# A lightweight convolution in front of a gated feed-forward: the first convolution by token steps, one cast moved, one pair of loads swapped

## The chip, the core and the metric

One NeuronCore of a Trainium2 chip runs the whole kernel in one launch. The metric is the device time of that launch in microseconds (us). Engines are named as the profile names them: PE is TensorE (matmuls; PEld are its weight loads), DVE is VectorE, ACT is ScalarE, POOL is GpSimd, SP is SyncE, which here only issues DMAs. A "q" behind an engine's name (SPq, POOLq) is its instruction queue, where DMA issues show. PSUM holds four tiles of 128 x 2 x 512 fp32 here; each is one buffer of a ring of four.

## The reference

Eight batches of 4096 tokens with 192 channels go through a causal convolution with 7 taps per head (8 heads of 24 channels, taps softmaxed), and the result through a feed-forward layer with a ReLU gate.

```python
w = softmax(weight)                                   # (8 heads, 7 taps)
out[b, s, h, g] = sum_k w[h, k] * x_pad[b, s + k, h, g]   # 6 zeros ahead of each sequence
x = out.reshape(32768, 192)
return (maximum(x @ w_gate, 0) * (x @ w_val)) @ w_out     # 192 -> 1536 -> 192
```

## The kernel before

**Units.** Batches b and b+4 are worked on as two streams; a unit `u` is 1024 tokens of both, two windows of 512 (`WIN`), and there are 16 units. A stream's channels lie in 64 partitions, so that the 128 partitions hold two streams; 192 channels are three chunks `c` of 64.

**Feed-forward.** For each unit and window, `gate_val` runs over `f`, the 12 blocks of 128 columns of `Wg` and `Wv`: twelve matmuls into two PSUM tiles, then ACT writes `gr` (ReLU), then DVE multiplies `gr` with the other tile into `hT`. For `f == 0` of the very first window the matmuls are ordered by chunk, so that chunk 0 can start before chunks 1 and 2 are there. `project_columns` multiplies by `Wo`.

**Convolution on PE (units 0 and 1).** x is cut into steps of 112 tokens; a step's matmul takes x itself as weights and a banded matrix of the taps (`bands[0]` for heads 0 to 3, `bands[1]` for heads 4 to 7) as moving data. `conv_dense(0, ...)` makes the first window: for each chunk in turn it takes one PSUM tile, does 40 matmuls (5 steps in the order `STEPS0` = 1, 0, 2, 3, 4, two heads' parts, two streams, two halves of the chunk) and evicts the tile to `xc[0]` (ACT for chunks 0 and 2, DVE for chunk 1). `conv_dense(1, [c])` makes the second window, one chunk ahead of each of the blocks f = 9, 10, 11 of the first window (`CONV1`). `conv(2)` and `conv(3)` make unit 1 in another form, with ACT copies into `y` and SP's DMA transposes into `xc[1]`.

**Convolution on the lane (units 2 to 14, here "the lane").** `lane_load(u)` loads a unit of x through POOL's queue into `x_e` (and, for unit 2, the last 16 tokens before it into `head`); `lane_turn(u)` has POOL copy `head` and `x_e` (into `turned` and `x_p`) and SP transpose them by DMA into `x_r`; ACT, DVE and POOL then form the sum over taps (`lane_first`, `product`, `lane_rest`, `add`). Unit 2's lane starts in unit 0, after `gate_val`, and its ACT and DVE work stands between unit 0's `gate_val` and unit 1's in the program order of these engines.

**The start.** SP loads the first window's x as five raw fp32 pieces (`load_raw`, order `STEPS0`); `cast` turns each into fp16: piece 1 half on POOL and half on ACT, pieces 0 and 2 on ACT, 3 and 4 on DVE. The weights are loaded by POOL's queue in five column slices (`load_w(0)` to `load_w(4)`, `Wg` and `Wv` each) into partitions 0 to 63 only; `both_halves` copies a slice to partitions 64 to 127: slices 0 and 1 on DVE, 2, 3 and 4 on POOL (`pool_halves`), and the last 256 columns by SP's DMA.

**What sets the order.** The schedule is manual: every engine runs its instructions in the order in which the program writes them. A tile framework puts in the semaphores. On POOL the order around the change is: four small fills (`ones`, two selects, `Z`, and `raw[0]`'s six zero rows, L160), the cast of piece 1's first half (L121), ten weight issues (L208), `pool_halves(2)` and `(3)` (L215), `load_x(1)` (L94, two issues), `pool_halves(4)`, `load_x(2)` (L94, two issues), `lane_load(2)` (L404 two issues, L415 one), the issue for `Wo` (L616), and then `lane_turn(2)`. `load_x(g)` loads the five steps of token group g for both streams, 2 x 5 x 128 rows of 192 elements; `lane_load` loads 2 x 8 x 128 such rows. On DVE the order is: band 0's eviction, the casts 3 and 4, the four copies for slices 0 and 1, the eviction of chunk 1, then `hT`. On ACT it is: the casts, `wn`, the cast of piece 2, band 1's eviction, the evictions of chunks 0 and 2, then `gr`. The three tiles of the first convolution are the first three buffers of the ring again, as in the order before the change.

Of the kernel before, what the change touches and what calls it, by code (L numbers as in the profile page):

```python
# [8 lines left out]
FP = mybir.dt.float32  # L9
# [6 lines left out]
def kernel(  # L16
# [12 lines left out]
    nc = tc.nc  # L29

    B, S, D = x.shape
    H, KW = weight.shape
    G = D // H
    DFF = moe_w_gate.shape[1]
    PAD = KW - 1
    NB = B // 2
    NCH = D // 64
    NBLK = D // 32
    NFF = DFF // 128
    WIN = 512  # L40
    NWIN = S // WIN
    SUB = 112
    STEPS = [4, 5, 4]
    TAPS = [(6, 5, 4), (3, 2), (1, 0)]
    GSUB = 5
    WARM = [2, 3, 1]
    STEPS0 = [1, 0, 2, 3, 4]
    CONV1 = [9, 10, 11]
# [8 lines left out]
    GROUPS = [(0, [WIN * w + SUB * j for j in range(GSUB)]) for w in range(2)]  # L57
    second = [min(t, 2 * UNIT - SUB) for t in range(UNIT, 2 * UNIT, SUB)]
# [11 lines left out]
    psum = ctx.enter_context(tc.tile_pool(name="psum", bufs=4, space=bass.MemoryType.PSUM))  # L70
# [5 lines left out]
    def staged(i, j):  # L76
        return stages[i][:, XH * j : XH * (j + 1)]

    def load_x(g, streams=range(2)):
# [22 lines left out]
    xts = {0: staged(0, 0).rearrange("p (j s d) -> p j s d", s=2, d=D)}  # L102
    ROWS = [SUB + PAD, 128, 128, 128, 80]
    raw = [
        apool.tile([128, FLAT - LDVE], FP, name=f"prod{jj + 1}")[:, 0 : 2 * D] for jj in range(GSUB)
    ]
# [10 lines left out]
            ),  # L117
        )

    def cast(copy, jj, lo=0, hi=2 * D):  # L120
        copy(  # L121
            out=xts[0][0 : ROWS[jj], jj, :, :].rearrange("p s d -> p (s d)")[:, lo:hi],
            in_=raw[jj][0 : ROWS[jj], lo:hi],
        )

    HR = 128 // H
# [35 lines left out]
    with nc.allow_low_precision("one of the terms is not zero"):  # L162
        nc.vector.tensor_reduce(
            out=Z[:, 112 : 112 + HR],
            in_=eye[:].rearrange("p (g i) -> p i g", i=HR),
# [4 lines left out]
        out=mask[:, :, 0],  # L170
        in_=eye[:].rearrange("p (g i) -> p g i", i=HR),
# [17 lines left out]
    for half in range(2):  # L189
        nc.tensor.matmul(  # L190
            out=raised[half][:, 0, 0 : SUB * H // 2],
            lhsT=zeros[:, 0:128],
            rhs=zeros[:, 0 : SUB * H // 2],
            start=True,
            stop=False,
            skip_group_check=True,
# [16 lines left out]
    def both_halves(copy, s, dst):  # L213
        cols = slice(HALVES[s], HALVES[s + 1])
        copy(out=dst[64:128, :, cols], in_=dst[0:64, :, cols])  # L215
# [2 lines left out]
        both_halves(nc.gpsimd.tensor_copy, s, Wg)  # L218
        both_halves(nc.gpsimd.tensor_copy, s, Wv)

    cast(nc.gpsimd.tensor_copy, 1, 0, D)
    for s in range(5):
        load_w(s)
    pool_halves(2)
# [6 lines left out]
        out=mx[:], in_=spread[:, 0, 0:KW], axis=mybir.AxisListType.X, op=ALU.max, negate=True  # L231
    )
    nc.scalar.activation(out=e[:, 0:KW], in_=spread[:, 0, 0:KW], func=ACTF.Exp, bias=mx[:])
    cast(nc.scalar.copy, 1, D)
    cast(nc.scalar.copy, 0)
    prod = const.tile([128, BW, KW], FP)
    z0 = Z[:, 112 - PAD : 113 - PAD]
# [2 lines left out]
        out=prod[:],  # L240
# [11 lines left out]
        out=blocks[:],  # L252
# [11 lines left out]
    for half, copy in enumerate((nc.vector.tensor_copy, nc.scalar.copy)):  # L264
        for j in range(128 // HR):
            s0 = HR * j - PAD
            lo, hi = max(0, -s0), min(BW, SUB - s0)
            nc.tensor.matmul(
                out=raised[half][:, 0, 0 : SUB * H // 2].rearrange("p (h t) -> p h t", t=SUB)[
                    :, :, s0 + lo : s0 + hi  # L270
                ],
                lhsT=Z[:, 112 - HR * j : 240 - HR * j],
                rhs=blocks[:, H // 2 * half : H // 2 * (half + 1), lo:hi],
                start=False,
                stop=(j == 128 // HR - 1),
                skip_group_check=True,
            )
        copy(
            out=bands[half][:].rearrange("p h t -> p (h t)"), in_=raised[half][:, 0, 0 : SUB * H // 2]
# [7 lines left out]
    for c in range(NCH):  # L287
        r0 = 0
        while r0 < 64:
            h = (64 * c + r0) // G  # L290
            r1 = min(64, G * (h + 1) - 64 * c)
            row = wn[HR * h : HR * h + 8, :]
            for st in range(2):
                nc.sync.dma_start(
                    out=tap[64 * st + r0 : 64 * st + r1, c, :],
                    in_=bass.AP(
                        tensor=row.tensor,
                        offset=row.offset,
                        ap=[row.ap[0], [0, (r1 - r0) // 8], [1, KW]],
                    ),  # L300
# [6 lines left out]
    def band(h):  # L307
        return bands[h // 4][0 : SUB + PAD, h % 4, :]

    xc = {}  # L310
# [3 lines left out]
    PLACE = {0: (0, 0, 0), 1: (0, 0, 1), 3: (0, 1, 0), 4: (0, 1, 1)}  # L314
    PLACE |= {6: (1, 0, 0), 7: (1, 0, 1), 2: (1, 1, 0), 5: (1, 1, 1)}

    def conv_dense(g, chunks):


        xt = xts[g]  # L320
        t0 = GROUPS[g][1][0]
        rows = SUB + PAD
        for c in chunks:
            ps = psum.tile([128, 2, 512], FP, name="ps")
            for jj in STEPS0:
                col = SUB * jj
                n = min(SUB, WIN - col)
                rows = n + PAD
                for second in range(2):
                    for st in range(2):  # L330
                        for k2 in range(2):
                            k = 2 * c + k2
                            h0, h1 = 32 * k // G, (32 * k + 31) // G
                            h, m = (h0, G * h1 - 32 * k) if second else (h1, 32)
                            p0 = 64 * st + 32 * k2
                            nc.tensor.matmul(
                                out=ps[p0 : p0 + m, 0, col : col + n],
                                lhsT=xt[0:rows, jj, st, 32 * k : 32 * k + m],
                                rhs=band(h)[0:rows, 0:n],
                                start=True,  # L340
                                stop=True,
                                tile_position=(0, p0),
                                skip_group_check=True,
                            )
            copy = nc.vector.tensor_copy if c == 1 and g == 0 else nc.scalar.copy
            copy(out=xc[0][:, c, t0 : t0 + WIN], in_=ps[:, 0, :])  # L346

    def conv(g):

# [47 lines left out]
    def lane_load(u):  # L397


        bp, t0 = u * UNIT // S, u * UNIT % S  # L400
        xe = epool.tile([128, TILES, 2, NCH, 64], F16, name="x_e")
        for st in range(2):
            row = (bp + NB * st) * S + t0
            nc.gpsimd.dma_start(  # L404
                out=xe[:, :, st, :, :].rearrange("p j c r -> p j (c r)"),
                in_=bass.AP(
                    tensor=x.tensor,
                    offset=x.offset + row * D,
                    ap=[[D, 128], [128 * D, TILES], [1, D]],
                ),  # L410
            )
        head = None
        if t0 and u - 1 not in xes and u - 1 not in xrs:
            head = const.tile([HALO, 2, NCH, 64], F16, name="head")
            nc.gpsimd.dma_start(  # L415
                out=head[:].rearrange("p s c r -> p s (c r)"),
                in_=bass.AP(
                    tensor=x.tensor,
                    offset=x.offset + (bp * S + t0 - HALO) * D,
                    ap=[[D, HALO], [NB * S * D, 2], [1, D]],  # L420
                ),
            )
        xes[u] = xe, head
# [95 lines left out]
    def gate_val(u, w):  # L519
        h = hpool.tile([128, NFF, 2, WIN], F16, name="hT")  # L520
        xcb = xc[u]
        for f in range(NFF):
            if u == 0 and w == 0 and f in CONV1:
                conv_dense(1, [CONV1.index(f)])
            pss = [psum.tile([128, 2, 512], FP, name="ps") for _ in range(2)]
            order = [(i, c) for i in range(2) for c in range(NCH)]
            if u == 0 and w == 0 and f == 0:
                order.sort(key=lambda ic: ic[1])
            for i, c in order:
                W = (Wg, Wv)[i]  # L530
                for st in range(2):
                    nc.tensor.matmul(  # L532
                        out=pss[i][:, st, :],
                        lhsT=W[64 * st : 64 * st + 64, c, 128 * f : 128 * (f + 1)],
                        rhs=xcb[64 * st : 64 * st + 64, c, WIN * w : WIN * (w + 1)],
                        start=(c == 0),
                        stop=(c == NCH - 1),
                        tile_position=(64 * st, 0),
                    )
            gr = gpool.tile([128, 2, WIN], F16, name="gr")  # L540
            nc.scalar.activation(out=gr[:], in_=pss[0][:], func=ACTF.Relu)  # L541
            nc.vector.tensor_tensor(out=h[:, f], in0=gr[:], in1=pss[1][:], op=ALU.mult)  # L542
        return h
# [62 lines left out]


    xc[0] = xcpool.tile([128, NCH, UNIT], F16, name="xc")
    both_halves(nc.vector.tensor_copy, 0, Wg)
    both_halves(nc.vector.tensor_copy, 0, Wv)  # L610
    both_halves(nc.vector.tensor_copy, 1, Wg)
    both_halves(nc.vector.tensor_copy, 1, Wv)
    conv_dense(0, range(NCH))
    xts[2] = load_x(2)
    lane_load(2)
    nc.gpsimd.dma_start(out=Wo[:], in_=moe_w_out.rearrange("(c p) d -> p c d", p=128))  # L616
    for u in range(NUNIT):
        lane = 1 <= u < NUNIT - 1
# [12 lines left out]
        if lane:  # L631
            for k in range(4 if u == 1 else 2, KW - 1):
                add(u + 1, k)
        hs = [gate_val(u, w) for w in range(2)]
        if lane:
            add(u + 1, KW - 1)
# [14 lines left out]
        for p in range(3):  # L651
            ps = project_columns(hs, p)
# [39 lines left out]
```

## Time and profile before

| what | value |
|---|---|
| median of 3 runs | 770.39 us (768.64 to 770.94) |
| the profiled execution's own time | 771.82 us |
| its span, first to last instruction | 770.1 us |
| PE busy | 761.8 us (99%) |
| DVE, ACT, POOL busy | 87%, 78%, 55% |
| granted PE clock | 1.0 |

The profile is of one execution, and its times count from the start of its span. A row of the timeline gives start, duration, engine, line, operation, tiles and count, and in brackets the idle time just before it with what ended it. A row of the chain of work that ended last gives start, duration and what the time went into. A "DMA share" is the mean busy share of the core's 16 DMA engines; it can be over 1 where transfers of one engine overlap.

### The profile page before, as it was taken

How to read it: one execution, taken by the hardware profiler on the slowest of the kernel's cores; microseconds unless marked ns; L12 is line 12 of the kernel's file. 1: busy time of each engine (PE TensorE's matmuls, PEld its weight loads, DVE VectorE, ACT ScalarE, POOL GpSimd, SP SyncE). 2: the span in 40 equal slices, each digit the busy share in tenths (PEclk: the TensorE clock that was granted, in tenths of full speed). 3: DMA queues.
4: the chain of work that ended last, by engine and by line, in shares of the span. 5: the costliest groups of instructions: out<-in, count | busy, mean ns of one | idle time of the engine just before them, and what ended most of it. 6: DMA issues, size and time to landing. Idle time of an engine off the chain costs nothing.

```text
span 770.1 us, 21550 instructions
## 1 busy us (share of the span) xinstructions
PE 761.8 (99%) x9402; PEld 380.9 (49%) x9402; DVE 669.9 (87%) x630; ACT 598.1 (78%) x622; POOL 423.1 (55%) x191
## 2 busy tenths in 40 slices
PE   8999999999999999999999999999999999999998
PEld 5454544444444444444444444444444444444448
DVE  6778989989899898989989899898998989996690
ACT  6788787978879787787878879788796877874471
POOL 8506839286490955919368292863919558191000
PEclk9999999999999999999999999999999999999999
DMA  8946919084290914709066190742909232040402
GB/s 131 127 78 106 124 28 141 2 113 53 56 112 3 140 26 80 87 3 149 18 97 70 23 144 2 116 51 48 118 3 133 33 76 50 2 83 2 83 2 83
DMA packets 123214, 53.79 MB, mean 70 GB/s; under 512 B 87648, under 2 KB 123120, under 8 KB 123120
## 3 DMA queue, kind: packets, MB, share of 16 engines
q1 hardware_dynamic: 86192, 38.06, 31.3%
q0 software_dynamic: 36768, 14.26, 17.8%
q8 instruction: 73, 1.20, 0.6%
q14 instruction: 21, 0.17, 0.1%
q10 hardware_dynamic: 160, 0.10, 0.0%
HBM read 29.40 MB, written 25.17 MB: 71 GB/s over the span
## 4 chain that ended last, share of the span: by engine, by line
PE 91%; POOL 3%; ACT 2%; DMA 1%; issue 1%; SPq 1%; DVE 0%; ACTq 0%; POOLq 0%
PE ps L532 60%; PE ps L552 28%; PE ps L588 2%; ACT prod L469 1%; SPq L443 1%; DMA Wg<-in_moe_w_gate_dram 1%; DMA x_r<-x_p 1%; POOL out_s L94 0%; POOL Wg L215 0%; POOL Wv L215 0%; POOL x_p L441 0%; DMA prod<-in_x_dram 0%; POOL x_e L404 0%; ACT out_s L371 0%; ACT acc L489 0%
## 5 line engine op out<-in xcount | busy, mean ns | idle before, releaser
L541 ACT ACTIVATE gr<-ps 128x1024 f16<-128x1024 f32 x384 | 392.6, 1023 | 146.7 <-PE ps L532 146.6
L542 DVE TENSOR_TENSOR hT<-gr,ps 128x1024 f16<-128x1024 f16 x384 | 468.6, 1221 | 42.2 <-ACT gr L541 15.8
L478 POOL TENSOR_TENSOR prod<-prod,prod 128x1792 f32<-128x1792 f32 x70 | 278.4, 3977 | 254.8 <-DVE prod L510 211.8
L532 PE MATMUL ps<-xc,Wg 64*128 64x512 f16 x2304 | 313.3, 376 | 2.0 <-DVE xc L346 1.0
L532 PE MATMUL ps<-xc,Wv 64*128 64x512 f16 x2304 | 312.8, 376 | 0.4 <-DVE hT L542 0.4
L552 PE MATMUL ps<-hT,Wo 128*32 128x512 f16 x4320 | 236.0, 379 | 0.0
L532 PEld LDWEIGHTS <-Wv 64*128 64x128 f16 x2304 | 131.0, 94 | 118.4 <-issue 1.2
L532 PEld LDWEIGHTS <-Wg 64*128 64x128 f16 x2304 | 113.3, 94 | 139.1 <-issue 8.9
L552 PEld LDWEIGHTS <-Wo 128*32 128x32 f16 x4320 | 114.1, 97 | 120.3 <-issue 6.3
L469 ACT ACTIVATE prod<-x_r,tap 128x1024 f32<-128x1024 f16 (+1 forms) x182 | 172.8, 1037 | 0.2 <-POOL xc L478 0.2
L500 DVE SCALAR_TENSOR_TENSOR acc<-x_r,tap,acc 128x1024 f32<-128x1024 f16 (+1 forms) x140 | 114.2, 873 | 5.6 <-ACT acc L489 5.6
L566 DVE STREAM_TRANSPOSE out_s<-ps 128x1024 f32<-128x1024 f32 x45 | 56.1, 1247 | 30.9 <-PE ps L552 30.8
L478 POOL TENSOR_TENSOR xc<-prod,prod 128x1792 f16<-128x1792 f32 x14 | 55.7, 3981 | 1.1
L441 POOL COPY x_p<-x_e 128x1536 f16<-128x1536 f16 x28 | 40.3, 1468 | 2.3 <-DMA x_e<-in_x_dram 2.3
L404 POOL DMA_DIRECT2D x_e<-in_x_dram x28 | 25.1, 901 | 4.2 <-POOL x_p L441 4.2
L489 ACT ACTIVATE acc<-x_r,tap 128x1024 f32<-128x1024 f16 (+1 forms) x28 | 21.5, 820 | 3.6 <-DMA x_r<-x_p 3.6
L500 DVE SCALAR_TENSOR_TENSOR xc<-x_r,tap,acc 128x1024 f16<-128x1024 f16 (+1 forms) x28 | 23.4, 877 | 0.0
L588 PE MATMUL ps<-Wo,hT 128*128 128x192 f16 x192 | 16.0, 246 | 0.0
L588 PEld LDWEIGHTS <-hT 128*128 128x128 f16 x192 | 15.8, 98 | 0.4 <-issue 0.4
L599 ACT COPY out_s<-ps 128x768 f32<-128x768 f32 (+2 forms) x5 | 3.2, 639 | 12.7 <-PE ps L588 12.7
L599 DVE COPY out_s<-ps 128x192 f32<-128x192 f32 x1 | 0.4, 358 | 13.3 <-PE ps L588 13.3
L510 DVE TENSOR_SCALAR prod<-x_r,tap 128x768 f32<-128x768 f16 x14 | 8.6, 612 | 0.0
(56 smaller groups left out, 61.3 us busy)
## 6 DMA issues: line engine op xcount, KB each, us to landing
out_dram<-out_s SPq DMA_DIRECT2D x63, 384.0 KB
x_e<-in_x_dram POOLq DMA_DIRECT2D x28, 384.0 KB, 10.2
x_r<-x_p SPq DMA_TRANSPOSE x112
out_s<-in_x_dram POOLq DMA_DIRECT2D x4, 240.0 KB, 5.6
prod<-in_x_dram SPq DMA_DIRECT2D x3, 192.0 KB
Wo<-in_moe_w_out_dram POOLq DMA_DIRECT2D x1, 576.0 KB, 11.7
out_s<-in_x_dram POOLq DMA_DIRECT2D x2, 192.0 KB, 4.9
Wg<-in_moe_w_gate_dram POOLq DMA_DIRECT2D x1, 240.0 KB, 5.7
```

What stands on the lines that cost most here:

```text
L404: nc.gpsimd.dma_start(out=xe[:, :, st, :, :].rearrange("p j c r -> p j (c r)"), in_=bass.AP(tensor=x.tensor, offset=x.offset + row * D, ap ...
L441: nc.gpsimd.tensor_copy(out=xp[:, :, :, st, :], in_=xe[:, :, st, :, :])
L469: nc.scalar.activation(out=prods[u, k][:, at - LDVE : at - LDVE + n], in_=shifted(u, c, k, t, n), func=ACTF.Copy, scale=tap[:, c, k : k + 1],)
L478: nc.gpsimd.tensor_tensor(out=p0[:] if k < KW - 1 else flat(u)[:, LDVE:FLAT], in0=p0[:], in1=prods.pop((u, k))[:], op=ALU.add,)
L489: nc.scalar.activation(out=accs[u][:, at : at + n], in_=shifted(u, c, 0, t, n), func=ACTF.Copy, scale=tap[:, c, 0:1],)
L500: nc.vector.scalar_tensor_tensor(out=(flat(u) if k == KW - 1 else acc)[:, at : at + n], in0=shifted(u, c, k, t, n), scalar=tap[:, c, k : k ...
L532: nc.tensor.matmul(out=pss[i][:, st, :], lhsT=W[64 * st : 64 * st + 64, c, 128 * f : 128 * (f + 1)], rhs=xcb[64 * st : 64 * st + 64, c, WI ...
L541: nc.scalar.activation(out=gr[:], in_=pss[0][:], func=ACTF.Relu)
L542: nc.vector.tensor_tensor(out=h[:, f], in0=gr[:], in1=pss[1][:], op=ALU.mult)
L552: nc.tensor.matmul(out=ps[32 * s : 32 * s + 32, b, :], lhsT=Wo[:, f, 64 * p + 32 * b : 64 * p + 32 * b + 32], rhs=hs[s // 2][:, f, s % 2, ...
L566: nc.vector.transpose(out=o[:, :, 64 * p : 64 * p + 64].rearrange("p t (b c) -> p b t c", b=2), in_=ps[:].rearrange("p b (t c) -> p b t c" ...
L588: nc.tensor.matmul(out=ps[:, i // 2, D * (i % 2) : D * (i % 2) + D], lhsT=h[:, f, st, 128 * q : 128 * (q + 1)], rhs=Wo[:, f, :], start=(f ...
```

## The change

Three things change, all of them in the first 30 us of the program's order.

1. The first convolution allocates its three PSUM tiles at once and runs by steps instead of by chunks: steps 1, 0, 2 of chunks 0, 1, 2, then step 3 of all chunks, then step 4 of all chunks. The number of matmuls stays 120. The three evictions stand at its end. On DVE, slice 0's two copies stand ahead of the eviction of chunk 1 and slice 1's two copies behind it. The function is split into `conv_steps` and `evict`; the second window's convolution uses the same two in the order that it had.
2. POOL casts nothing: ACT casts the whole of piece 1. POOL's ten weight issues then follow its small fills directly.
3. On POOL's queue `lane_load(2)` (with `head`) stands ahead of `load_x(2)`.

```diff
-    cast(nc.gpsimd.tensor_copy, 1, 0, D)
     for s in range(5):
         load_w(s)
...
-    cast(nc.scalar.copy, 1, D)
+    cast(nc.scalar.copy, 1)
     cast(nc.scalar.copy, 0)
...
-    def conv_dense(g, chunks):
...
-        for c in chunks:
-            ps = psum.tile([128, 2, 512], FP, name="ps")
-            for jj in STEPS0:
...
-            copy = nc.vector.tensor_copy if c == 1 and g == 0 else nc.scalar.copy
-            copy(out=xc[0][:, c, t0 : t0 + WIN], in_=ps[:, 0, :])
+    def conv_steps(g, ps, c, steps):
+        for jj in steps:
...
+    def evict(copy, g, ps, c):
+        copy(out=xc[0][:, c, WIN * g : WIN * (g + 1)], in_=ps[:, 0, :])
...
             if u == 0 and w == 0 and f in CONV1:
-                conv_dense(1, [CONV1.index(f)])
+                c = CONV1.index(f)
+                ps = psum.tile([128, 2, 512], FP, name="ps")
+                conv_steps(1, ps, c, range(GSUB))
+                evict(nc.scalar.copy, 1, ps, c)
...
     xc[0] = xcpool.tile([128, NCH, UNIT], F16, name="xc")
+    first = [psum.tile([128, 2, 512], FP, name="ps") for _ in range(NCH)]
+    for steps in (STEPS0[:3], STEPS0[3:4], STEPS0[4:]):
+        for c in range(NCH):
+            conv_steps(0, first[c], c, steps)
     both_halves(nc.vector.tensor_copy, 0, Wg)
     both_halves(nc.vector.tensor_copy, 0, Wv)
+    for c, copy in enumerate((nc.scalar.copy, nc.vector.tensor_copy, nc.scalar.copy)):
+        evict(copy, 0, first[c], c)
     both_halves(nc.vector.tensor_copy, 1, Wg)
     both_halves(nc.vector.tensor_copy, 1, Wv)
-    conv_dense(0, range(NCH))
+    lane_load(2)
     xts[2] = load_x(2)
-    lane_load(2)
     nc.gpsimd.dma_start(out=Wo[:], in_=moe_w_out.rearrange("(c p) d -> p c d", p=128))
```

More of the change, by code (lines that the diff above doesn't have):

```diff
@@ L118, in load_raw, with cast @@
         )
-    def cast(copy, jj, lo=0, hi=2 * D):
+    def cast(copy, jj):
         copy(
-            out=xts[0][0 : ROWS[jj], jj, :, :].rearrange("p s d -> p (s d)")[:, lo:hi],
-            in_=raw[jj][0 : ROWS[jj], lo:hi],
+            out=xts[0][0 : ROWS[jj], jj, :, :].rearrange("p s d -> p (s d)"),
+            in_=raw[jj][0 : ROWS[jj], :],
         )
@@ L315 @@
     PLACE |= {6: (1, 0, 0), 7: (1, 0, 1), 2: (1, 1, 0), 5: (1, 1, 1)}
-    def conv_dense(g, chunks):
-        xt = xts[g]
-        t0 = GROUPS[g][1][0]
-        rows = SUB + PAD
-        for c in chunks:
-            ps = psum.tile([128, 2, 512], FP, name="ps")
-            for jj in STEPS0:
[L326 to L344, printed above, removed]
-            copy = nc.vector.tensor_copy if c == 1 and g == 0 else nc.scalar.copy
-            copy(out=xc[0][:, c, t0 : t0 + WIN], in_=ps[:, 0, :])
@@ new lines, in conv_steps @@
+    def conv_steps(g, ps, c, steps):
+        for jj in steps:
+            col = SUB * jj
+            n = min(SUB, WIN - col)
+            rows = n + PAD
+            for second in range(2):
+                for st in range(2):
+                    for k2 in range(2):
+                        k = 2 * c + k2
+                        h0, h1 = 32 * k // G, (32 * k + 31) // G
+                        h, m = (h0, G * h1 - 32 * k) if second else (h1, 32)
+                        p0 = 64 * st + 32 * k2
+                        nc.tensor.matmul(
+                            out=ps[p0 : p0 + m, 0, col : col + n],
+                            lhsT=xts[g][0:rows, jj, st, 32 * k : 32 * k + m],
+                            rhs=band(h)[0:rows, 0:n],
+                            start=True,
+                            stop=True,
+                            tile_position=(0, p0),
+                            skip_group_check=True,
+                        )
```

## The prediction

> **What bounds the kernel now.** I read the page's engine row first, then PE's waits and the timeline where PE stands still, and then the chain of work that ended last, for the first 72 us.
>
> ```profile
> PE 761.8 (99%) x9402; PEld 380.9 (49%) x9402; DVE 669.9 (87%) x630; ACT 598.1 (78%) x622; POOL 423.1 (55%) x191
> ```
>
> PE is busy in 761.8 of 770.1 us. The change takes no work off PE, so only PE's standstills can be won.
>
> The timeline places them, each with its wait in brackets:
>
> ```profile
> 9.64 0.39 PE L532 MATMUL ps<-xc,Wg 64*128 64x512 f16 x2 [1.01 <-DVE xc L346]
> 10.50 0.83 PE L532 MATMUL ps<-xc,Wg 64*128 64x512 f16 x6
> 12.17 0.33 PEld L532 LDWEIGHTS <-Wg 64*128 64x128 f16 x5 [0.50 <-POOL Wg L215]
> 12.94 0.33 PEld L532 LDWEIGHTS <-Wv 64*128 64x128 f16 x5 [0.44 <-POOL Wv L215]
> 21.46 0.23 PE L336 MATMUL ps<-band,out_s 118*32 118x112 f16 x2
> 22.63 0.63 PE L336 MATMUL ps<-band,out_s 118*32 118x112 f16 x38 [0.94 <-DMA out_s<-in_x_dram]
> 61.80 0.82 PE L532 MATMUL ps<-xc,Wg 64*128 64x512 f16 x6
> 65.71 0.82 PE L532 MATMUL ps<-xc,Wg 64*128 64x512 f16 x6 [0.96 <-ACT gr L541]
> 66.97 0.82 PE L532 MATMUL ps<-xc,Wv 64*128 64x512 f16 x6 [0.43 <-DVE hT L542]
> ```
>
> PE first waits for chunk 1 (until 9.64), then for POOL's copies of slice 2 (12.17, 12.94), then for the second window's x, which `load_x(1)` brings (22.63), and last in unit 1 for ACT and DVE, 0.96 + 0.43 = 1.39 us. So two stretches matter: up to 22.63, which ends with a landing, and up to 66.97. The chain tells what sets both:
>
> ```profile
> 3.44 0.47 POOL out_s L121
> ...
> 6.62 4.54 DMA Wg<-in_moe_w_gate_dram
> ...
> 11.30 0.82 POOL Wg L215
> ...
> 15.07 1.73 POOL out_s L94 x2
> ...
> 19.03 1.66 POOL out_s L94 x2
> ...
> 24.06 7.66 issue
> ...
> 35.21 1.59 SPq L443
> ...
> 44.75 4.04 DMA x_r<-x_p
> ...
> 64.64 1.03 ACT gr L541
> ```
>
> It is one POOL chain: weight issues, slice 2's landing (11.16), POOL's copies, `load_x(1)` at 15.07, the loads behind it, the landing of `head` (31.7), POOL's copies, SP's transposes, `x_r` (seen by ACT at 49.10), ACT's products, and the late `gr` at 64.64.
>
> **The cast off POOL (term A).** POOL's last fill ends at 1.88 + 0.41 = 2.29 us, and its weight issues begin at 3.91, behind the wait for piece 1 and the cast:
>
> ```profile
> 1.88 0.41 POOL L160 MEMSET prod<- 6x384 f32 x1
> 3.40 0.99 ACT L121 CAST out_s<-prod 128x192 f16<-128x192 f32 x2
> 5.57 0.51 ACT L121 CAST out_s<-prod 128x384 f16<-128x384 f32 x1 [0.85 <-DMA prod<-in_x_dram]
> ```
>
> All ten issues can come 3.91 - 2.29 = 1.6 us earlier. On ACT the first of the two casts in 0.99 grows to the 0.51 of a full one, by some 0.03 to 0.16 us; `wn` and the tap issues behind it on SP shift by that. The taps' first reader is ACT at 49.10, and the two `both_halves` issues behind them on SP feed f = 10 and 11, so this costs nothing.
>
> How much of the 1.6 us lasts until slice 2 lands? The x pieces (SP's queue, q1) and the weights (POOL's, q0) share the DMA engines. The rows are of the view of DMA queues (packets, MB, share of the engines' time), in this order for 0 to 4.0 us, 4.0 to 5.2, 5.5 to 8.1 and 24 to 31; a row of POOL's issues from the timeline stands last:
>
> ```profile
> q1 hardware_dynamic: 677, 0.49, 43.9%
> q1 hardware_dynamic: 458, 0.33, 89.1%
> q0 software_dynamic: 839, 0.20, 86.3%
> q0 software_dynamic: 3052, 1.15, 147.9%
> 6.62 0.63 POOL L208 DMA_DIRECT2D Wg<-in_moe_w_gate_dram  x1
> ```
>
> x nearly alone takes a share of 0.89, the first weights nearly alone 0.86, and a longer stretch later 1.48. So 0.9 isn't the ceiling; both at full rate would want 1.75, and at 1.48 each keeps 85%. The first weights move 839 / 2.6 = 323 packets per us, hardly more than POOL hands out (an issue of 64 x 3 rows takes 0.63 us, 305 per us): that stretch waits for the issues, and an earlier issue pays. At 85% during the overlap I take 1.2 us of the 1.6 as kept. The bounds are 0 (the slowest engine never idle, total work the same) and 1.6; it is nearer the upper because of the 1.48.
>
> It could be less: if an engine serves the two queues in turn and overlaps nothing, a pair of packets costs 16 x 0.89 / 382 = 37 ns (x: 458 / 1.2 per us) plus 16 x 0.863 / 323 = 43 ns, so either queue gets 200 per us instead of 323. Some 500 of the 1152 x rows are left at 4.0 us (q1's first row, less its few other packets) and take until 6.5; 268 of the 768 rows of slices 0 and 1 remain then and end at 7.3 instead of 8.1. That keeps 0.8 us: a rival of its own below. (The Trainium skill, "DMA: Bandwidth & Descriptors", section "Queues, rings and completion order", says that each DMA engine takes turns between the queues that have work, a packet at a time, which speaks for this price; no row here shows both queues busy for long enough to bear it out.)
>
> x pieces that come later: piece 2 delays ACT's cast and, behind it, band 1's eviction; pieces 3 and 4 delay DVE's casts and, behind them, slice 0's copies. By the turns the last x row comes 1.1 us later, step 4 is cast at about 8.0, and the convolution ends at 8.4. PE has this to spare, as the next part shows.
>
> **The convolution by steps.**
>
> ```profile
> 6.31 1.78 PE L336 MATMUL ps<-band,out_s 118*32 118x112 f16 x120 [0.18 <-DVE band L278]
> 7.24 0.58 ACT L346 CAST xc<-ps 128x512 f16<-128x512 f32 x1 [0.72 <-PE ps L336]
> 8.34 0.58 ACT L346 CAST xc<-ps 128x512 f16<-128x512 f32 x1 [0.52 <-PE ps L336]
> 8.58 0.28 DVE L215 COPY Wv<-Wv 64x384 f16<-64x384 f16 x1
> 8.90 0.69 DVE L346 CAST xc<-ps 128x512 f16<-128x512 f32 x1
> ```
>
> The same 120 matmuls end at 8.1. Chunk 0 loses: its eviction moves from 7.24 to about 8.1. Chunk 1 wins: it now stands ahead of slice 1's copies on DVE (8.58), so it runs 8.2 to 8.9 instead of 8.90 to 9.59. ACT evicts chunk 2 at 8.7 to 9.3. PE does f = 0 chunk by chunk at (10.50 - 9.64) / 2 = 0.43 us each: 8.75, 9.18, 9.61, and f = 1 starts at 10.05 instead of 10.50. Slice 1's copies (4 x 0.28 us for both slices) are now queued behind the eviction, 8.9 to 9.5, in time for f = 1. With slice 2's copies 1.2 us earlier (done at 10.9 and 11.7) f = 2 at 11.35 no longer waits. A block takes 12.88 / 10 = 1.29 us:
>
> ```profile
> 29.05 12.88 DVE L542 TENSOR_TENSOR hT<-gr,ps 128x1024 f16<-128x1024 f16 x10 [0.75 <-ACT gr L541]
> ```
>
> So PE reaches the second window's convolution at 10.05 + 8 x 1.29 = 20.4 instead of 21.46.
>
> But there it needs `load_x(1)`'s second stream, which lands 22.63 - 1.2 = 21.4 if it moves with POOL's chain. **So the step order alone is worth nothing here; the landing decides, and term A is 1.2 us.** Without the head start the wait at 22.63 would merely grow. From the other side, PE's own path allows at most about 22.63 - 20.6 = 2.0, if the load lands earlier still (it would move partly ahead of SP's copies of the last columns).
>
> **The lane's load first (term B).** `head` and `x_e` leave POOL's queue 1.66 us earlier in issue and no longer stand behind the 1280 rows of `load_x(2)`: 3052 / 7 = 436 rows per us makes 2.9 us. With A, `head` lands at 31.7 - 4.1 = 27.6, and `turned`, `x_p`, the transposes (35.21 becomes 31.1) and `x_r` (49.10 becomes 45.0) follow. ACT is free of `conv(2)`'s copies at 49.10 - 2.33 = 46.77, in the new frame 45.6, so its wait of 2.33 us goes:
>
> ```profile
> 44.11 1.03 PE L358 MATMUL ps<-out_s,band 118*112 118x240 f16 x8
> 45.07 5.36 PE L552 MATMUL ps<-hT,Wo 128*32 128x512 f16 x96
> 49.10 1.55 ACT L489 ACTIVATE acc<-x_r,tap 128x1024 f32<-128x1024 f16 x2 [2.33 <-DMA x_r<-x_p]
> 62.63 1.24 DVE L566 STREAM_TRANSPOSE out_s<-ps 128x1024 f32<-128x1024 f32 x1
> Wo<-in_moe_w_out_dram POOLq DMA_DIRECT2D x1, 576.0 KB, 11.7
> ```
>
> PE asks for the first `gr` of unit 1 about 0.9 us after 61.80, at 62.7; ACT gives it at 64.64, 1.9 late. Winning 2.3 covers that. DVE, fed by the same accumulators, is free after its last transpose (62.63) at about 63.6, which then waits for PE alone; it is then just in time, so I leave 0.1 and count **1.3 of the 1.39 us**. Bounds: 0, if `x_r` isn't earlier, and 1.39.
>
> What moves back is `load_x(2)`: two issues behind three others, landing by about 31.7, where `lane_load(2)` landed. `conv(2)` reads it at 44.11: 12 us of cover. `Wo` keeps its place; it lands 11.7 us after its issue at 23.0 and is read at 45.07. `load_x(3)`'s issues come earlier with the POOL copies and cost nothing.
>
> **Sum.** 1.2 + 1.3 = 2.5 us off the profiled 771.82 gives 769.3. That execution lies 1.4 us above the median of the runs; the same 2.5 off 770.39 gives 767.9.
>
> **Rivals.**
> 1. *Engines take turns between the queues* (above): A is 0.8, and the time 770.39 - 2.1 = 768.3.
> 2. *The head start is lost*: the slowest DMA engine was never idle, slice 2 lands at 11.1 as before. For it: the landing took 4.54 us after the issue. Against: the issue-limited rate. Only B stays: 769.1; with some of A, 768.7.
> 3. *The lane isn't earlier* (something else holds ACT): A alone, 769.2. Against: the chain goes through that wait.
> 4. *Slower: SP's transposes collide with loads.* They now start at 31.1, while `Wo` and `load_x(2)` still move. SP's transposes are spread between
>
> ```profile
> L443 SPq DMA_TRANSPOSE x_r<-x_p x8: 1246/1254/1594, 35.2 to 44.7; - x8
> L390 SPq DMA_TRANSPOSE xc<-out_s x10: 1175/1252/2023, 46.8 to 65.1; - x10
> ```
>
> 1.25 and 2.02 us an issue. Eight at 2.02 from 31.1 and a landing of 4.04 give 51.3, against 47.9 for an `x_r` that keeps its place relative to PE: 3.4 us lost on ACT, 1.2 won by A, 772.6. It turns from gain to loss where 31.1 + 8s + 4.04 passes 49.10, at s = 1.75. Against: the old transposes ran into `load_x(3)` and seven of the eight kept near 1.25.
>
> **How the numbers follow.** Chances: forecast 0.45; turns 0.17; head start lost 0.14; lane not earlier 0.10; collision 0.14. About 0.3%, 2.3 us, is what can be told from no change, so faster means under 768.1: the forecast lies just beyond that, and with A between 1.0 and 2.0 its own range is 767.1 to 768.1, so nearly all of it counts (0.42); half of the turns (0.08) and a little of the others (0.02) make it 0.52. Slower by that, over 772.7, is the collision's worse part, 0.09; between lies 0.39. The range goes from 766.4 (A at 2.0, B at 1.39, and 0.6 for the spread of the runs) to 770.6 (half of the collision left out, and nothing won).
>
> **What would show it.** POOL's first weight issue at about 2.3; slice 2's copy at about 10.1 instead of 11.30; f = 1 on PE at about 10.1; the convolution of the second window resuming at about 21.4 with a wait of about 0.8; `turned` at about 27.6 instead of 31.74; no wait of ACT ahead of `acc`; no PE wait for `gr` in unit 1. It is wrong if slice 2's copies don't move, if x pieces come so late that the convolution ends after 9.5, if the transposes stretch beyond 1.75 us, or if PE meets a new wait behind 67 us.

## The result, and the profile after

| | before | after |
|---|---|---|
| median, 7 runs each | 770.63 us (768.64 to 772.18) | 768.55 us (767.80 to 768.68) |
| profiled execution, its own time | 771.82 us | 768.63 us |
| its span | 770.1 us | 766.9 us |

The ratio is 0.9973, with a 95% interval of 0.9961 to 0.9985: 2.1 us less, a shade under the 0.3% that the prediction took as the bound. The two profiled executions lie 3.2 us apart.

The engine row and PE's waits of the changed kernel, from the page and from the view of waits:

```profile
PE 761.4 (99%) x9402; PEld 378.6 (49%) x9402; DVE 670.9 (87%) x630; ACT 598.6 (78%) x622; POOL 422.9 (55%) x190
```

```profile
PE ps L180 <- DVE e L136: 1.3, 1, 1.3
PE ps L530 <- ACT xc L341: 0.6, 1, 0.6
PE ps L530 <- DVE hT L540: 0.2, 1, 0.2
```

PE's work is the same, and the waits for the second window's x and for unit 1's `gr` and `hT` are gone. The timeline of the changed kernel at the places that the prediction named:

```profile
2.25 0.85 POOL L208 DMA_DIRECT2D Wg<-in_moe_w_gate_dram  x1
6.61 0.77 DVE L121 CAST out_s<-prod 128x384 f16<-128x384 f32 x2 [0.43 <-DMA prod<-in_x_dram]
8.55 1.07 ACT L341 CAST xc<-ps 128x512 f16<-128x512 f32 x2 [1.87 <-PE ps L330]
8.79 0.82 POOL L215 COPY Wg<-Wg 64x768 f16<-64x768 f16 x1
10.48 0.83 PE L530 MATMUL ps<-xc,Wg 64*128 64x512 f16 x6
12.81 0.82 PE L530 MATMUL ps<-xc,Wv 64*128 64x512 f16 x6 [0.21 <-DVE hT L540]
21.34 0.64 PE L330 MATMUL ps<-band,out_s 118*32 118x112 f16 x40
25.86 0.62 POOL L430 COPY turned<-head 16x192 f16<-16x192 f16 x2 [3.87 <-DMA head<-in_x_dram]
29.33 11.15 SPq L438 DMA_TRANSPOSE x_r<-x_p  x8
45.33 1.59 ACT L484 ACTIVATE acc<-x_r,tap 128x1024 f32<-128x1024 f16 x2
60.51 0.82 PE L530 MATMUL ps<-xc,Wg 64*128 64x512 f16 x6
64.41 0.81 PE L530 MATMUL ps<-xc,Wg 64*128 64x512 f16 x6
```

and one further row of before, unit 1's fourth block:

```profile
67.61 0.83 PE L532 MATMUL ps<-xc,Wg 64*128 64x512 f16 x6
```

The 3.2 us of this pair come in two steps. Unit 1 starts at 60.51 instead of 61.80, which is 1.29 us, and its fourth block at 64.41 instead of 67.61, which is 1.91 us more. From there on the two keep that distance. Of the 1.29 us only some 0.1 lies ahead of the second window's convolution (21.34 against 21.46); the rest is before's wait there, until 22.63. The chain that ended last tells how the work moved:

```profile
6.46 2.06 PE ps L330 x89
8.53 0.02 issue
8.55 0.60 ACT xc L341
9.15 0.04 issue
9.19 1.27 PE ps L530 x10
10.46 0.02 issue
10.48 1.03 ACT gr L539
11.52 0.02 issue
11.54 1.23 DVE hT L540
12.77 0.04 issue
12.81 8.59 PE ps L530 x78
```

Before, the chain ran through POOL, a landing, SP's transposes and ACT up to 66.97. Now it is PE's own from 12.81 on. Just ahead of that lies one detour: block f = 2 needs the PSUM tile that `hT` of f = 0 gives back at 12.77.

### The profile page after: what moved, and what is told of

The parts are those of the page before. It is cut to its first block, busy times and chain, and to the rows that moved or that the text cites. A ratio compares the mean times of both kernels' runs of the same rounds, so it can differ in the third digit from the quotient of the medians.

```text
span 766.9 us, 21548 instructions
## 1 busy us (share of the span) xinstructions
PE 761.4 (99%) x9402; PEld 378.6 (49%) x9402; DVE 670.9 (87%) x630; ACT 598.6 (78%) x622; POOL 422.9 (55%) x190
## 4 chain that ended last, share of the span: by engine, by line
PE 99%; ACT 0%; POOL 0%; DVE 0%; issue 0%; POOLq 0%
PE ps L530 65%; PE ps L550 31%; PE ps L586 2%; PE ps L330 0%; PE ps L353 0%; PE ps L180 0%; DVE hT L540 0%; ACT gr L539 0%; PE ps L267 0%; PE ps L190 0%; ACT xc L341 0%; PE ps L186 0%; POOL prod L160 0%; POOL rows L144 0%; ACT out_s L597 0%
## 5 line engine op out<-in xcount | busy, mean ns | idle before, releaser
L530 PEld LDWEIGHTS <-Wg 64*128 64x128 f16 x2304 | 111.2, 94 | 138.8 <-issue 6.9
```

The source lines that it names most:

```text
L530: nc.tensor.matmul(out=pss[i][:, st, :], lhsT=W[64 * st : 64 * st + 64, c, 128 * f : 128 * (f + 1)], rhs=xcb[64 * st : 64 * st + 64, c, WI ...
```

## The experiments

The theories: (1) the end is the later of two chains, PE's path up to the second window's convolution and the lane's chain; (2) two independent sums, A and B. Beside them stood the question what the order by steps is worth. The first six kernels are the other six combinations of the three parts.

**The cast alone.**

```diff
-    cast(nc.gpsimd.tensor_copy, 1, 0, D)
...
-    cast(nc.scalar.copy, 1, D)
+    cast(nc.scalar.copy, 1)
```

> The kernel before with only the cast of piece 1 taken off POOL. Theory 1 (the end is the later of two chains: PE's own path up to the second window's convolution, and the lane's chain POOL, head, transposes, ACT products): POOL's chain comes about 2.1 us earlier as in the changed kernel, the second window no longer makes PE wait, PE gains 1.3 to 1.6 us up to 23 us, and its wait in unit 1 shrinks because the lane's chain gains more than PE: in all about 2 us, 768.6. Theory 2 (two independent sums, A = 1.3 and B = 1.9): A alone, 769.3, with the full waits of unit 1. On the step order: theory 1 expects f = 1 to start at about 10.1 here, earlier than the changed kernel's 10.48, since chunk 0 is evicted while PE still works on chunks 1 and 2, and slice 1's copies are done before chunk 1's tile is; the rival, that late x pieces hurt the order by chunks more, expects 10.9 or later.

Measured: 768.84 us, ratio 0.9981 (0.9971 to 0.9990). Its times lie in two groups, seven at 767.98 to 768.86 and five at 769.91 to 770.43; the profiled execution (770.43) is of the upper one. Its timeline:

```profile
10.21 0.83 PE L531 MATMUL ps<-xc,Wg 64*128 64x512 f16 x6
21.06 0.64 PE L335 MATMUL ps<-band,out_s 118*32 118x112 f16 x40
29.28 0.62 POOL L434 COPY turned<-head 16x192 f16<-16x192 f16 x2 [7.01 <-DMA head<-in_x_dram]
47.71 1.55 ACT L488 ACTIVATE acc<-x_r,tap 128x1024 f32<-128x1024 f16 x2 [2.50 <-DMA x_r<-x_p]
64.33 0.82 PE L531 MATMUL ps<-xc,Wg 64*128 64x512 f16 x6 [0.97 <-ACT gr L540]
65.58 0.82 PE L531 MATMUL ps<-xc,Wv 64*128 64x512 f16 x6 [0.43 <-DVE hT L541]
```

The wait for the second window is gone. But although `turned` came 2.46 us earlier than before and PE only 1.6, ACT's wait for `x_r` is longer, 2.50 us. Theory 1 in its plain form can't give that, and theory 2 doesn't give the lower group. By the times, the loss is there in full or not at all; no execution of the lower group was profiled.

**The lane's load first, alone.**

```diff
-    xts[2] = load_x(2)
     lane_load(2)
+    xts[2] = load_x(2)
```

> The kernel before with only the lane's load ahead of the third group's load. Both theories: head lands about 2.9 us earlier (turned at about 28.8 instead of 31.74), ACT no longer waits for x_r, the waits of unit 1 go; everything up to 23 us as before, the wait at 22.6 included. 768.7. If head isn't earlier without the cast's head start, 770.4.

Measured: 769.00 us, ratio 0.9982 (0.9973 to 0.9991). Its timeline:

```profile
10.36 0.82 POOL L215 COPY Wg<-Wg 64x768 f16<-64x768 f16 x1
21.76 0.63 PE L336 MATMUL ps<-band,out_s 118*32 118x112 f16 x38 [0.17 <-DMA out_s<-in_x_dram]
27.16 0.62 POOL L435 COPY turned<-head 16x192 f16<-16x192 f16 x2 [3.97 <-DMA head<-in_x_dram]
45.75 1.59 ACT L489 ACTIVATE acc<-x_r,tap 128x1024 f32<-128x1024 f16 x2
```

ACT no longer waits. Slice 2's copy stands at 10.36, directly behind POOL's issues and without a wait; the 11.30 in the profile of before was a late landing of that one execution. So the usual gate there is POOL's own issuing, and the cast's head start goes through whole: 8.68 to 8.89 in all nine profiles without POOL's cast whose issues start at 2.25, 10.33 to 10.46 in the other three with it.

**The order by steps alone.** The edit is the change's without those of the cast and the swap.

```diff
+    first = [psum.tile([128, 2, 512], FP, name="ps") for _ in range(NCH)]
+    for steps in (STEPS0[:3], STEPS0[3:4], STEPS0[4:]):
+        for c in range(NCH):
+            conv_steps(0, first[c], c, steps)
...
+    for c, copy in enumerate((nc.scalar.copy, nc.vector.tensor_copy, nc.scalar.copy)):
+        evict(copy, 0, first[c], c)
...
-    conv_dense(0, range(NCH))
```

> The kernel before with only the first convolution by steps and its evictions at the end. Theory 1: f = 1 may start at about 10.1 instead of 10.5, but POOL's copies and the second window's landing at 22.6 take that back: 770.4, no change, with longer waits there. Rival (the step order carries the gain up to 23 us): 769.3.

Measured: 770.95 us, ratio 0.9999 (0.9990 to 1.0009): nothing. Its timeline:

```profile
9.99 0.83 PE L531 MATMUL ps<-xc,Wg 64*128 64x512 f16 x6
21.66 0.63 PE L331 MATMUL ps<-band,out_s 118*32 118x112 f16 x38 [0.59 <-DMA out_s<-in_x_dram]
47.98 1.55 ACT L485 ACTIVATE acc<-x_r,tap 128x1024 f32<-128x1024 f16 x2 [2.18 <-DMA xc<-out_s]
```

f = 1 starts at 9.99, as the prediction's step said (10.05), and the later waits take it back: for the second window, for `x_r`, and 0.8 us at 112 us, where PE waits for DVE in this profile alone. The view names `xc<-out_s` as the end of ACT's wait; the tile that ACT reads is `x_r`, whose last landing came at 47.67.

**Both POOL changes, by chunks; and the two left pairs.**

These put two of the three edits above together each.

> Both POOL changes without the convolution by steps. Theory 1: as the changed kernel or up to 0.4 us better, since f = 1 starts at about 10.1 and nothing else waits: 768.2. Rival (the order by steps is needed to bear the late x pieces): f = 1 at 10.9 or later, 769.0.

> The changed kernel with half of piece 1's cast back on POOL. Theory 1: as the swap alone, 768.7: the wait for the second window stays at 22.6, the waits of unit 1 are gone. If the step order were worth something of its own, 768.2.

> The changed kernel with the third group's load ahead of the lane's load again. Theory 1 (later of two chains): PE as in the changed kernel up to 60 us, the lane's chain only about 2.1 us earlier than before, so that PE's loss in unit 1 falls from 1.9 us to about 1.1: 768.9 to 769.7. Theory 2 (independent sums): the full 1.9 us lost in unit 1, 769.5 to 770.4.

| parts | median us | ratio to before (95%) | its times |
|---|---|---|---|
| cast, swap | 768.12 | 0.9967 (0.9955 to 0.9979) | 767.91 to 768.44 |
| steps, swap | 769.17 | 0.9989 (0.9978 to 1.0000) | ten at 768.62 to 769.80, two at 772.25 and 772.26 |
| cast, steps | 769.25 | 0.9992 (0.9981 to 1.0002) | six at 767.96 to 768.63, six at 769.87 to 771.09 |

The steps add nothing to either part. With the cast and without the swap the two groups are there again. With the swap most times lie together, but not all: the swap alone has one at 770.93, and the steps with the swap have the two at 772.25 and 772.26. One of these two was profiled: there PE waits for the second window until 23.45.

```profile
23.45 0.63 PE L331 MATMUL ps<-band,out_s 118*32 118x112 f16 x38 [1.98 <-DMA out_s<-in_x_dram]
```

**What makes a landing late.** The traces record each of the 16 landings that a DMA counts, and the packets of the queue that the view of DMA queues calls `instruction` (q8, 16 KB each, 6 to 13 us apart in the first 70 us, 0.9 to 1.6 us each). In us:

```
the last x_r transpose     15 landings      the 16th   instruction packet: start, takes
before                     46.99 to 47.11    48.79      46.72  1.04
cast alone                 45.32 to 45.44    47.39      45.08  1.29
cast, steps                45.27 to 45.39    46.82      44.72  1.04
after                      41.47 to 41.59    41.60      45.41  1.13

second window, stream 1
before                     20.56 to 21.55    22.59      20.08  0.95
steps, swap                20.15 to 21.33    23.41      20.95  0.98
after                      17.82 to 19.36    19.55      19.20  1.01
```

Where the last transpose lands as an instruction packet moves, one of the 16 landings comes 1.4 to 2.0 us behind the others, and ACT waits for it. The trace doesn't say on which engine a packet ran, so I made a third theory, the instruction fetch, and tried it: `x_r` is made later in the changed kernel, by work that does nothing new.

```diff
-        for st in range(2):
+        for st in ([0] * 3 if u == 2 else []) + [0, 1]:
             nc.gpsimd.tensor_copy(out=xp[:, :, :, st, :], in_=xe[:, :, st, :, :])
```

with 2, 3 and 5 extra copies.

> The changed kernel with the lane's x_r made later by 2.9 us (POOL does the first of unit 2's two x_p copies three times instead of once, 1.43 us each). The last x_r transpose then lands at about 41.6 + 2.9 = 44.5, still ahead of ACT's end of the conv(2) copies (45.3). Both theories: no change, 768.5.

> The changed kernel with x_r 4.3 us later (two further copies beyond the first extra one). The last transpose's data then ends at about 45.8, landing near 45.9. Theory of the plain landing: ACT waits 0.6 us, which its slack in unit 1 covers: 768.5 to 768.8. Theory of the instruction fetch (one DMA engine is held for about 1 us by a 16 KB instruction packet that is fetched as ACT ends the conv(2) copies, and with it the last of 16 landings of x_r): ACT waits 1.5 to 2.3 us and PE loses 1.1 to 1.9: 769.6 to 770.5, in some or all runs.

> The changed kernel with x_r 7.2 us later: landing at about 48.8, ACT waits about 3.4 us. Both theories: PE loses that less the slack of about 0.4 that the kernel before shows (a wait of 2.33 cost it 1.92): about 3 us, 771.5. It gives the price of a us of x_r away from the fetch.

Three extra copies: 770.90 us, all eleven runs between 770.57 and 771.54, ratio to before 1.0003 (0.9993 to 1.0014). The timeline, and the DMA queue view of 45.7 to 46.7 us:

```profile
34.65 10.32 SPq L438 DMA_TRANSPOSE x_r<-x_p  x8
48.07 1.55 ACT L484 ACTIVATE acc<-x_r,tap 128x1024 f32<-128x1024 f16 x2 [2.73 <-DMA xc<-out_s]
```

```profile
q1 hardware_dynamic: 105, 0.02, 12.4%
q8 instruction: 1, 0.02, 5.8%
```

ACT ended its copies at 48.07 - 2.73 = 45.34. Fifteen landings came by 46.08, the sixteenth at 47.76; the packet started at 45.74. ACT starts 0.31 us behind the last landing (48.07 - 47.76), so a plain landing would have cost a wait of about 1.05 us; it was 2.73, and the kernel lost the whole of what it had won: 2.3 us. This is what the fetch theory said, somewhat above its upper end. (The view again names `xc<-out_s`; the landing at 47.76 is that of `x_r`.)

Five extra copies: 774.70 us, 3.2 us above what both theories expected. In its profile `turned` itself came at 27.49, the last landing at 50.42 and so ACT's wait was not 3.4 but 5.35 us. The price was off too. With waits of 2.2 to 2.7 us (five profiles) PE loses about 0.4 us less than ACT waits; here, matmul by matmul against the changed kernel, it loses 6.3 us between 45 and 66 us, 1 us more than ACT waits. It also waits for DVE's `out_s`, which reads PSUM tiles that PE needs back (a row of the timeline, then two of the view of waits):

```profile
50.73 1.55 ACT L484 ACTIVATE acc<-x_r,tap 128x1024 f32<-128x1024 f16 x2 [5.35 <-DMA x_r<-x_p]
PE ps L530 <- DVE out_s L564: 1.7, 1, 1.7
PE ps L550 <- DVE out_s L564: 1.1, 1, 1.1
```

Two extra copies: 770.21 us, not the 768.5 that both expected, with times spread from 768.06 to 772.07, ratio 0.9995 (0.9980 to 1.0009). In the profiled execution (772.06) ACT doesn't wait for `x_r`; PE lost its time earlier, where the edit has no part:

```profile
23.24 0.80 PE L330 MATMUL ps<-band,out_s 118*32 118x112 f16 x38 [2.18 <-DMA out_s<-in_x_dram]
48.80 1.59 ACT L484 ACTIVATE acc<-x_r,tap 128x1024 f32<-128x1024 f16 x2
```

Fifteen landings there came by 21.91, the last at 23.20. `x_r` was later than expected as well: `turned` came at 27.59, and the landings at 46.90 and 47.55 instead of 44.5, behind the 45.3 at which ACT is free in the changed kernel. So the expectation of no change had lost its ground. What part of the spread is `x_r`'s and what the second window's, this run doesn't tell.

The packets of the transposes settle more of the third theory. The last `x_r` transpose ends with 32 packets of 4 bytes, and the landings follow them. In the five profiles with a 16 KB packet in the way (the three of the table, the steps alone and three extra copies) thirty of them start on time, and the last two start within 0.02 us of the end of the instruction packet: in before at 47.74 and 47.76, where the packet ends at 47.76. In six others the sixteenth landing is 0.65 to 1.22 us behind, and there 8 KB packets of the other instruction queue (q14) lie in the way; in five of the six the last two 4-byte packets again start at the end of one of them. In the three that are left no instruction packet moves in the 2 us ahead, and the sixteenth landing is 0.01 us behind or less.

So the instruction packet holds the last packets back. What it doesn't explain is that in those five profiles the late landing comes 1.0 to 1.1 us after its packets, where the other fifteen take about 0.3. For the second window the pattern isn't there: an instruction packet starts 0.3 to 3.5 us ahead of its last landing in all fourteen profiles, and the sixteenth is 1.0 us or more behind in three of them.

**Weights a little later.** Both POOL changes, by chunks, with the fill of six rows done three times, so that the weight issues start at 3.17.

```diff
     nc.gpsimd.memset(raw[0][0:PAD, :], 0.0)
+    nc.gpsimd.memset(raw[0][0:PAD, :], 0.0)
+    nc.gpsimd.memset(raw[0][0:PAD, :], 0.0)
```

> Both POOL changes without the order by steps, and POOL's fill of six rows done three times, so that the weight issues start at about 3.0 instead of 2.25. If the x pieces 3 and 4 are late because the weights share the DMA engines with them, DVE casts them earlier (wait of 0.8 shrinks to about 0.3), the first convolution ends about 0.4 us earlier and f = 1 starts at about 9.5 instead of 9.91; slice 2 still lands before PE asks for it. 767.7 against 768.1. If something else delays the pieces: 768.1, unchanged.

Measured: 768.74 us, ratio 0.9977 (0.9966 to 0.9987), so no gain. Its timeline:

```profile
6.51 0.78 DVE L121 CAST out_s<-prod 128x384 f16<-128x384 f32 x2 [0.59 <-DMA prod<-in_x_dram]
9.90 0.83 PE L533 MATMUL ps<-xc,Wg 64*128 64x512 f16 x6
21.46 0.63 PE L337 MATMUL ps<-band,out_s 118*32 118x112 f16 x38 [0.48 <-DMA out_s<-in_x_dram]
```

The casts of pieces 3 and 4 start at 6.09 to 6.24 in the four kernels with POOL's cast and at 6.43 to 6.90 in the other profiles: the weights do hold the x pieces, by about half a us. The 6.51 here lies within that range, so it isn't shown that a later start helps. f = 1 didn't move (9.91 in the same kernel without the fills), and PE waits 0.48 us for the second window, whose load POOL now issues later.

**The changed kernel and the one by chunks, side by side.**

> The changed kernel once more, beside the next one on the same chip. Two theories of the spread. If the second window's x is held by an instruction packet on one DMA engine only where its landing falls behind that packet (about 19.2 to 20.2 us), the changed kernel, whose landing lies on the edge, has most of its runs at 768.0 to 768.7 and some at 769.5 to 772. If the first sample of 7 runs (767.8 to 768.7) is the whole of it, no run lies above 769.

> The changed kernel without the convolution by steps (both POOL changes kept), beside the changed kernel on the same chip. If the order by steps costs its 0.4 us at the start (f = 1 at 9.91 against 10.48): 0.3 to 0.5 us below the changed kernel's fast runs. If that was chance: equal.

Measured on the same chip: 768.59 us both, ratios 0.9978 (0.9969 to 0.9987) and 0.9968 (0.9958 to 0.9978), times 768.20 to 769.38 and 768.03 to 770.62. f = 1 starts, in the profiles of by steps and by chunks:

```profile
10.09 0.83 PE L530 MATMUL ps<-xc,Wg 64*128 64x512 f16 x6
```

```profile
10.20 0.82 PE L531 MATMUL ps<-xc,Wg 64*128 64x512 f16 x6
```

So the 0.57 us between 10.48 and 9.91 in the first two profiles belong to those two executions and not to the order. No version beat the changed kernel clearly; the one by chunks does the same with less change.

## Why the prediction was right

The time, 768.55, lies 0.65 us above the forecast of 767.9 and inside the range; a gain of 2.1 us stands against 2.5 forecast. It isn't under the 768.1 from which the prediction spoke of faster (0.52); the case between (0.39) came. The time of the first rival, 768.3, lies nearer to the measured one than the forecast, but not for that rival's reason, as the second point shows. The steps:

- *POOL's weight issues at 2.3, slice 2's copy at 10.1*: 2.25 and 8.79. The head start is 1.6 us and was kept whole, where the forecast took 1.2, since POOL's queue and not the landing is the usual gate (10.33 to 10.46 in the three other profiles with its cast). The distance from 11.30 is larger only because before's profiled execution had a late landing there.
- *Engines taking turns between queues*: the end points came out, the rates did not. The last rows of slices 0 and 1 start at 7.30 (7.3 by that price, 8.1 before), and the last x row starts at 6.43 (6.5 by that price, 5.95 before, so half a us later and not the 1.1 of the prediction). But the first weight row moved at 4.41 and not by 4.0, and from then until 6.43 the trace has 377 x rows and 583 weight rows, 187 and 289 per us, where the price gave each 200; that these errors cancel is luck. It didn't decide term A, since slice 2 came with the full head start. The rule of turns (the Trainium skill, "DMA: Bandwidth & Descriptors", "Queues, rings and completion order") agrees with the trace in so far as the x queue fell from 89.1% of the engines' time between 4.0 and 5.2 us to the first row below while the second moved beside it; equal shares no row here shows:

```profile
q1 hardware_dynamic: 342, 0.25, 73.0%
q0 software_dynamic: 101, 0.02, 20.9%
```

- *Term A, 1.2 us, set by the second window's landing*: 1.29 us in the profiled pair, but the step that names the limit was wrong, and the size is luck. The load came in time and PE's own path set the end: convolution to 8.5 instead of 8.1, f = 1 at 10.48 instead of 10.05, and a wait of 0.21 us for `hT` of f = 0 that I hadn't seen behind POOL's copies. "f = 2 no longer waits" was wrong. The wait that went was before's for a sixteenth landing 1.04 us behind the fifteenth (22.59 and 21.55). In the swap alone, where it is 0.78 us behind, PE keeps POOL's cast and ends only 0.41 us behind the changed kernel's profile; by medians the cast adds some 0.4 to 0.9 us to the swap, not 1.2.
- *The order by steps is worth nothing*: right, shown alone, with each other part, and side by side.
- *Term B: `turned` at 27.6, no wait of ACT, no wait for `gr`*: 25.86, none, none. `turned` came 5.9 us earlier and not 4.1; the swap alone moves it by 4.6 (27.16), where 2.9 was counted. Alone, the swap is worth 1.4 us (0.7 to 2.1). In the pair it was 1.91 instead of 1.3, since I counted the two bracketed waits only and not PE's shift from block to block. The cause was incomplete: ACT's 2.33 us before were for the most part the sixteenth landing, 1.68 us behind the others (48.79 - 47.11). Moving `x_r` by some 5.5 us takes it out of reach of that; moving it by 1 to 2, as the cast alone does, is a matter of luck.
- *The sum*: 3.2 us in the profiled pair against 2.5, but 2.1 between medians. I took the losses of one execution off the median of others. That execution was 1.2 us above the median of its kernel, and three late landings stand in it: slice 2's, the second window's and that of `x_r`. How many a typical one has, one profile can't tell.
- *Rivals*: "head start lost", "lane not earlier" and the collision didn't happen; the eight transposes took 11.15 / 8 = 1.39 us each, well below the 1.75 from which they would have cost something.

Shown: the three parts' worth, that an `x_r` landing put back to 46 us loses all of the gain with one landing late, and, by the packets' times, that an instruction packet holds that landing's last packets. Open: why such a landing then takes some 0.7 us longer than the others, and what delays the second window's sixteenth landing. No run took the instruction packets away.

## What to carry to other kernels

A wait that ends in a landing ends, in these traces, with the last of 16, which may come 1 to 2 us behind the rest; look when the landing falls, not only how long the wait is, and move the load clear of the edge rather than just ahead of it. When two chains meet at one consumer, a gain on one is worth at most the slack of the other, so test the parts alone and in pairs before giving either the credit. The profile is of one execution: take its waits off its own time, and look for rows in it (a copy that waits for a landing at 11.30 where it otherwise follows its queue at 10.4) that other executions of the same code don't have.

## What I hadn't expected of the hardware

A 16 KB packet of the instruction queue comes every 6 to 13 us in the first 70 us and takes 0.9 to 1.6 us. In the five profiles where the last landings of `x_r` fell near one, 15 of 16 were within 0.12 us and the last was 1.4 to 2.0 us behind. Clear of it a landing isn't safe either: 8 KB packets of the other instruction queue (q14) go with a lag of 0.65 to 1.22 us in six profiles. The changed kernel shows both cases: in its first profile all 16 landings came within 0.13 us, in its second the last came at 42.72, 1.22 us behind (41.50), with such a packet until 41.68. Neither costs anything, as ACT isn't free before 44.9. That fits the spread of the times, without being shown to be its cause: before spans 768.4 to 773.6 us over all runs, the changed kernel 767.8 to 769.4 over 18.
